# Attention and an MLP on one core: w_out's last quarter in two halves, fewer blank matmuls, and a new order written out as one list

## The chip, the core and the metric

The kernel runs on one core of a Trainium2 chip. The time is that of the device, in microseconds (us) from the start to the end of one execution; the number to compare is the median over repeated runs. The engines are TensorE (PE in the profile, with its weight loads as PEld), VectorE (DVE), ScalarE (ACT), GpSimd (POOL) and SyncE (SP), which here only issues transfers.

## The reference

```
# q, k, v: 8 batches x 8 heads x 576 tokens x 64, float32
def phi(x): r = max(x, 0); return concat([r * cos_w, r * sin_w], -1)   # 128 features
q_p, k_p = phi(q), phi(k)
kv  = einsum('bhsf,bhsd->bhfd', k_p, v)
z   = sum(k_p, axis=2)
num = einsum('bhsf,bhfd->bhsd', q_p, kv)
den = einsum('bhsf,bhf->bhs', q_p, z)[..., None] + 1e-06
x   = (num / den).transpose(0, 2, 1, 3).reshape(4608, 512)
h   = x @ w_in                       # 512 x 2048
out = max(0.01 * h, h) @ w_out       # 2048 x 512
```

`cos_w` and `sin_w` depend on the token's place alone. All inputs and the output are float32; the kernel multiplies in float16.

## The kernel before

The 4608 tokens are worked off in nine groups of 512: the main part of each batch is one group (0 to 7), and the eight batches' last 64 tokens are the ninth. All of w_in (512 x 2048) and w_out (2048 x 512) are loaded in float32 through staging tiles and cast to float16 once; w_in comes in eight pieces (`load_w1(i, cp)`), w_out in four quarters of 128 partitions x 2048 elements (`load_w2(i)`, staging tile `w2st`), each with one cast, `cast_w2(i, eng)`.

A batch goes through these steps. `q_prep` (later `q_part`) makes phi's cosine and sine parts of q (`qp`), `k_pair` (later `k_part`) those of k (`kp`), and `v_pair` (later `v_main`, `v_tail`) casts v, with a column of ones that yields z. In batches 0 and 1 TensorE turns q with a matmul against an identity (`q_turn` into `ps_qt`, `q_turned` copies it out to `qpT`); later a transposing transfer does it. `kv_half` multiplies k and v for one half of the heads (`ps_kvh`), `kv_half_copy` takes it to `kv`; `num_half` multiplies with q (`ps_numh`), `num_div` takes out the denominator (`den`), its reciprocal (`rden`), and divides (`xp`); `x_turn` and `x_turned` turn x into `xT`.

The MLP of group 0 begins in four quads (`quad`), while w_in is still arriving, and goes on in plain products of 512 columns (`ffn1`, eight matmuls a call, `ffn1_out` being the activation on ScalarE; then `ffn2` against w_out, a quarter of its rows a call). Group 1's first product is plain too (`f1_pair`, L833). From group 2 on w_in's product, and from group 1 on w_out's, are made by a scheme with seven block products for eight: `p1` (L882) and `p2` (L975) are groups of four matmuls of 256 columns on sums of blocks that VectorE makes ahead (`w1_sums`, `x_sums`, `g_sums`, `w2_sums`). Between these products PSUM banks are emptied on ScalarE (`seed`, `u_copy`, `lrelu`, `u_lrelu`, `o_copy`) and VectorE (`u_add`, `o_add`). `o_store` sends an output tile out.

TensorE also multiplies blanks: `idle(n, where)` issues n matmuls of a zero tile, 512 columns each, into a PSUM tile `ps_idle` that nobody reads (L190). 19 of them stand ahead of q's first turn, then seven, and eight.

What sets the order: each engine works off its instructions in the order in which the program issues them. The start, up to group 0's `ffn2_out`, is code written out call by call. The rest is a list of calls (`line`), each with a number from the tables in `PLACE`, and is issued in the order of these numbers; `ON` holds a letter for each call that can go to VectorE or ScalarE. Tiles come from pools: an operation that takes a tile of a pool waits until the tile's last reader is done. All loads go through SP's one queue, in program order.

Of the kernel before, what the change touches and what calls it, by code (L numbers as in the profile page):

```python
# [9 lines left out]
dt = mybir.dt  # L10
# [4 lines left out]
J = 4  # L15


@with_exitstack
def kernel(
# [75 lines left out]
    def staged(shape, name, soon=False):  # L95
# [3 lines left out]
    def load_main(nm, src, b, parts=(0, 1), soon=False):  # L99

        if parts[0] == 0:
            st[nm, b] = staged([P, H, J, D], f"{nm}st", soon)
        lo, hi = 4 * parts[0], 4 * parts[-1] + 4
        nc.sync.dma_start(
            st[nm, b][:, lo:hi],
            src[b, lo:hi, 0:MAIN, :].rearrange("h (p j) d -> p h j d", j=J),
        )

    def load_kvtail(nm, src, b):

        t = kvtail.tile([P, H // 2, D], dt.float32, name=f"{nm}tl", tag="kvtail")
        v4 = src[b, :, MAIN:S, :].rearrange("(c o) p d -> o p c d", o=2)
        for o in range(2):
            nc.sync.dma_start(t[o * TAIL : (o + 1) * TAIL], v4[o])
        st[nm + "t", b] = t

    def load_qtail(i):
        if "qt" not in st:
            st["qt"] = staged([P, J, H, D], "qtl")
        for o in range(2):  # L120
            nc.sync.dma_start(
                st["qt"][o * TAIL : (o + 1) * TAIL, i],
                q[2 * i + o, :, MAIN:S, :].rearrange("h p d -> p h d"),
            )

    def load_pair(nm, src, b, lo, hi):
# [3 lines left out]
        flat = src[b].rearrange("h s d -> (h s d)").rearrange("(c x e) -> x c e", x=P, e=JP * D)  # L130
# [3 lines left out]

    def load_k(b):
        load_main("k", k, b)
        load_kvtail("k", k, b)

    def load_v(b):
        load_main("v", v, b)  # L140
        load_kvtail("v", v, b)
# [12 lines left out]
    def load_w1(i, cp):  # L154
# [11 lines left out]
    load_main("q", q, 0, (0,))  # L166
    load_pair("k", k, 0, 0, 1)
    load_pair("k", k, 0, 1, 2)
    load_main("q", q, 0, (1,))
    load_pair("k", k, 0, 2, 4)  # L170
    load_pair("v", v, 0, 0, 2)
    load_pair("v", v, 0, 2, 4)
    load_w1(0, 0)
    load_w1(1, 0)
    load_w1(0, 1)
    load_w1(1, 1)
    load_w1(3, 0)
    load_w1(3, 1)
    load_w1(2, 0)
    load_w1(2, 1)  # L180

    blank = early.tile([P, MAIN], dt.float16, name="blank", tag="blank", bufs=1)
    nc.vector.memset(blank, 0.0)
# [8 lines left out]
    idle(11)  # L192

    ident32 = early.tile([P, P], dt.float32, name="ident32", tag="ident32", bufs=1)
    make_identity(nc, ident32)
    ident = const.tile([P, P], dt.float16, name="ident")
    nc.vector.tensor_copy(ident, ident32)
    w_ang = math.pi / 2.0 / S  # L200
    half_pi = const.tile([P, 1], dt.float32, name="half_pi")
    nc.vector.memset(half_pi, math.pi / 2.0)
    eps = const.tile([P, 1], dt.float32, name="eps")
    nc.vector.memset(eps, 1e-6)
    zero = const.tile([P, 1], dt.float32, name="zero")
    nc.vector.memset(zero, 0.0)
    NA = J + 1 + JP
    pos = const.tile([P, NA], dt.float32, name="pos")
    nc.gpsimd.iota(
        pos[:, 0:J],  # L210
        pattern=[[1, J]],
        base=0,
        channel_multiplier=J,
        allow_small_or_imprecise_dtypes=True,
    )
    for o in range(2):
        nc.gpsimd.iota(
            pos[o * TAIL : (o + 1) * TAIL, J : J + 1],
            pattern=[[1, 1]],
            base=MAIN,  # L220
            channel_multiplier=1,
            allow_small_or_imprecise_dtypes=True,
        )
        nc.gpsimd.iota(
            pos[o * TAIL : (o + 1) * TAIL, J + 1 : NA],
            pattern=[[1, JP]],
            base=0,
            channel_multiplier=JP,
            allow_small_or_imprecise_dtypes=True,
        )  # L230
    cos_t = const.tile([P, NA], dt.float32, name="cos_t")
    sin_t = const.tile([P, NA], dt.float32, name="sin_t")
    nc.scalar.activation(cos_t, pos, AF.Sin, bias=half_pi, scale=w_ang)
    nc.scalar.activation(sin_t, pos, AF.Sin, bias=zero, scale=w_ang)
    warm = const.tile([P, 1], dt.float16, name="warm")
    nc.scalar.activation(warm, zero, AF.Lrelu)

    ones = const.tile([P, H, J, 2], dt.float32, name="ones")
    nc.vector.memset(ones, 1.0)
    vmain = const.tile([P, H, J, NE], dt.float16, name="vmain")  # L240
    nc.vector.tensor_copy(vmain[:, :, :, D:NE], ones)
    vtail = const.tile([P, H // 2, 2, NE], dt.float16, name="vtail")
    nc.gpsimd.memset(vtail, 0.0)
    for o in range(2):
        sl = slice(o * TAIL, (o + 1) * TAIL)
# [671 lines left out]
    def f1_all(g):  # L917
# [16 lines left out]
        if sets == 4:  # L934
            return
# [406 lines left out]
```

## Time and profile before

| | before |
|---|---|
| median of 3 runs | 270.19 us (269.72, 270.19, 270.2) |
| span of the profiled execution | 268.3 us |
| TensorE busy | 262.5 us (98%), 2715 matmuls |
| VectorE busy | 209.2 us (78%) |
| ScalarE busy | 198.6 us (74%) |
| GpSimd busy | 7.7 us (3%) |
| granted TensorE clock | 1.000 |
| chain that ended last | PE 82%, DMA 13%, SP's queue 3%, DVE 1% |

A row of a timeline gives the start, the duration, the engine, the line, the operation with what it writes and reads, the shapes and how many alike follow one another; in brackets stands the idle time just ahead and who ended it. A row of the chain gives the start, the duration and what it was. Of the profiled execution only the span is known, from the first to the last instruction; the time of a run is the longer by what lies around it.

### The profile page before, as it was taken

What the parts mean: (1) busy time and instruction counts of PE and PEld (TensorE: products, weight loads), DVE (VectorE), ACT (ScalarE), POOL (GpSimd) and SP (SyncE); (2) the same over time, 40 slices, a digit from 0 to 9 for tenths busy, and PEclk for the clock granted to TensorE, in tenths of its full rate; (3) what the DMA queues carried; (4) which work ended last, traced back from release to release, by engine and by line L of the source; (5) the groups of instructions that cost most, each with busy time, mean ns of one, the idle gap of its engine ahead of it and who ended that gap; (6) DMA issues with size and microseconds to landing.
All of it is one profiled execution on the core that took longest, in us unless ns stands there. A gap on an engine that the chain in (4) does not pass through costs nothing.

```text
span 268.3 us, 6694 instructions
## 1 busy us (share of the span) xinstructions
PE 262.5 (98%) x2715; PEld 222.9 (83%) x2715; DVE 209.2 (78%) x436; ACT 198.6 (74%) x336; POOL 7.7 (3%) x20
## 2 busy tenths in 40 slices
PE   8999999999999999999999999999999999999994
PEld 3585455566999999999999999999998999999983
DVE  4894998997998998889979967897876674746641
ACT  7675545787989999689878967984996666785621
POOL 2121011000000000000000000000000000000000
PEclk9999999999999999999999999999999999999999
DMA  6999999999999999989899999798893623200116
GB/s 207 377 385 399 380 411 365 276 249 281 209 304 254 234 240 245 264 199 222 221 231 238 198 293 255 140 181 151 135 204 22 138 43 125 112 2 0 78 36 201
DMA packets 82654, 57.05 MB, mean 213 GB/s; under 512 B 54464, under 2 KB 75968, under 8 KB 82112
## 3 DMA queue, kind: packets, MB, share of 16 engines
q1 hardware_dynamic: 82320, 56.37, 84.0%
q8 instruction: 21, 0.34, 0.5%
q10 hardware_dynamic: 304, 0.26, 0.3%
q14 instruction: 9, 0.07, 0.1%
HBM read 36.70 MB, written 9.44 MB: 172 GB/s over the span
## 4 chain that ended last, share of the span: by engine, by line
PE 82%; DMA 13%; SPq 3%; DVE 1%; POOL 0%; issue 0%
PE ps_o L975 34%; PE ps_h L882 18%; PE ps_s L882 14%; DMA w2st<-in_moe_w_out_dram 6%; PE ps_h L833 5%; DMA w1st<-in_moe_w_in_dram 4%; PE ps_num L418 3%; DMA kpr<-in_k_dram 3%; PE ps_kv L317 2%; SPq L131 2%; PE ps_h L975 2%; PE ps_o L543 1%; PE ps_s L975 1%; PE ps_kv L324 1%; DVE w L265 0%; SPq L163 0%
## 5 line engine op out<-in xcount | busy, mean ns | idle before, releaser
L975 PEld LDWEIGHTS <-g 128*128 128x128 f16 x640 | 62.1, 98 | 6.8
L268 DVE TENSOR_TENSOR u<-ps_s,u 128x512 f32<-128x512 f32 x56 | 38.5, 687 | 19.3 <-PE ps_s L882 18.4
L882 PEld LDWEIGHTS <-w 128*128 128x128 f16 x448 | 48.7, 114 | 1.0
L975 PE MATMUL ps_o<-w,g 128*128 128x256 f16 x352 | 46.8, 273 | 0.0
L902 ACT COPY u<-ps_h 128x512 f32<-128x512 f32 x56 | 32.8, 589 | 6.3 <-PE ps_h L882 6.0
L882 PEld LDWEIGHTS <-wa 128*128 128x128 f16 x336 | 34.4, 106 | 1.9
L882 PE MATMUL ps_h<-xw,w 128*128 128x256 f16 x224 | 32.5, 273 | 0.0
L975 PE MATMUL ps_o<-wb,g 128*128 128x256 f16 x232 | 31.5, 273 | 0.0
L909 ACT ACTIVATE g<-u 128x1024 f16<-128x1024 f32 x28 | 29.6, 1060 | 2.3 <-DVE u L268 2.3
L975 PEld LDWEIGHTS <-gs 128*128 128x128 f16 x256 | 24.6, 98 | 2.6
L994 ACT COPY ob<-ps_o 128x512 f32<-128x512 f32 (+1 forms) x32 | 18.0, 561 | 6.0 <-PE ps_o L975 5.8
L892 ACT COPY ps_s<-ps_h 128x512 f32<-128x512 f32 x28 | 16.2, 579 | 6.2 <-PE ps_h L882 5.7
L895 ACT ACTIVATE g<-ps_s 128x512 f16<-128x512 f32 x28 | 16.8, 601 | 5.1 <-PE ps_s L882 4.8
L895 ACT ACTIVATE g<-ps_h 128x512 f16<-128x512 f32 x28 | 16.7, 600 | 5.3 <-PE ps_h L882 5.1
L436 DVE TENSOR_TENSOR xs<-ps_num,rden 128x512 f16<-128x512 f32 x28 | 19.4, 691 | 1.5
L268 DVE TENSOR_TENSOR ob<-ps_o,ob 128x512 f32<-128x512 f32 (+1 forms) x22 | 14.8, 672 | 3.3 <-PE ps_o L975 2.1
L882 PE MATMUL ps_s<-xT,wa 128*128 128x256 f16 x112 | 16.8, 273 | 0.0
L882 PE MATMUL ps_h<-xw,wa 128*128 128x256 f16 x112 | 16.8, 273 | 0.0
L882 PE MATMUL ps_s<-xw,wa 128*128 128x256 f16 x112 | 16.8, 273 | 0.0
L882 PE MATMUL ps_s<-xT,w 128*128 128x256 f16 x112 | 16.8, 273 | 0.0
L882 PE MATMUL ps_h<-xT,w 128*128 128x256 f16 x112 | 16.7, 273 | 0.0
L975 PE MATMUL ps_o<-wb,gs 128*128 128x256 f16 x120 | 16.5, 273 | 0.0
(121 smaller groups left out, 434.5 us busy)
## 6 DMA issues: line engine op xcount, KB each, us to landing
out_dram<-ob SPq DMA_DIRECT2D x16, 512.0 KB, 3.4
qst<-in_q_dram SPq DMA_DIRECT2D x7, 1024.0 KB, 7.0
kst<-in_k_dram SPq DMA_DIRECT2D x6, 1024.0 KB, 8.1
vst<-in_v_dram SPq DMA_DIRECT2D x6, 1024.0 KB, 6.8
w1st<-in_moe_w_in_dram SPq DMA_DIRECT2D x8, 512.0 KB, 11.6
w2st<-in_moe_w_out_dram SPq DMA_DIRECT2D x4, 1024.0 KB, 13.3
vpr<-in_v_dram SPq DMA_DIRECT2D x4, 576.0 KB, 10.7
kpr<-in_k_dram SPq DMA_DIRECT2D x3, 576.0 KB, 11.1
```

The source lines that it names most:

```text
L131: nc.sync.dma_start(st[nm, b][:, lo:hi].rearrange("p c j d -> p c (j d)"), flat[:, lo:hi])
L268: nc.vector.tensor_tensor(out=o, in0=a, in1=b, op=ALU.add)
L418: nc.tensor.matmul(ps[lo:hi, h // 4, (h % 4) * NE : (h % 4) * NE + NM], lhsT=qpT[:, h, lo:hi], rhs=kv[b][:, h, 0:NM],)
L436: nc.vector.tensor_tensor(out=xs, in0=ps[:, :, 0 : 4 * NE].rearrange("p a (b e) -> p a b e", e=NE)[:, :, :, 0:D], in1=rden.rearrange("p (a ...
L833: nc.tensor.matmul(ps, lhsT=w1[m // 4][c // 2][:, c % 2, m % 4 : 512 : 4], rhs=st["xT", g][:, c], start=(c == 0), stop=(c == NKC - 1),)
L882: nc.tensor.matmul(bank[:, p], lhsT=w(c), rhs=x_blocks(g)[n][:, c], start=(fresh and p == 0 and c == 0), stop=(c == 1), skip_group_check=True,
L892: nc.scalar.copy(bank1[bj], bank1[bi])
L895: nc.scalar.activation(st["g" + nm, g][:, 2 * t : 2 * t + 2], bank1[bi], AF.Lrelu)
L902: nc.scalar.copy(st["u", g, t][:, n], bank1[bi])
L909: nc.scalar.activation(st["gt", g][:, :, 1, 2 * t : 2 * t + 2], st["u", g, t], AF.Lrelu)
L975: nc.tensor.matmul(bank, lhsT=st[G2[n], g][:, m, pair * P : (pair + 1) * P], rhs=W2[n](m), start=(fresh and m == 0), stop=(m == NH - 1), s ...
L994: nc.scalar.copy(o_at(g, half_, col, pair), bank_of(bi, pair, pair is None))
```

## The change

The same work is issued in another order, and in finer pieces.

- One text, `ORDER`, lists every call of the program from the first load to the last store, and a loop looks each name up and calls it. The letter at an entry's end names the engine (A ScalarE, V VectorE, G GpSimd). `num_div` is now three entries (`den`, `rec`, `xdiv`; in the halves `hden`, `hrec`, `hdiv`), `kv` is `kv_mm` and `kv_copy`, and loads of tails go by half.
- The last quarter of w_out is loaded in two halves of 128 x 1024 (`ldw2 3 0 2`, `ldw2 3 2 4`) and cast in two, the first on VectorE, the second on ScalarE. The second quarter's cast goes from VectorE to ScalarE.
- Ahead of q's first turn stand 13 blanks (11 and 2) and not 19; the later ones are in pairs between the turns (27 blanks in all, 34 before).
- GpSimd casts no part of batch 0's v (VectorE takes three of the four, ScalarE one) and one piece of w_in, not two; it still casts two parts of batch 1's v.
- TensorE's matmuls other than blanks are the same ones. VectorE has 3 instructions more, ScalarE 1 more, GpSimd 3 fewer.

The core of the diff:

```
-    def load_w2(i):
-        t = staged([P, 4, DM], "w2st", i > 1)
-        nc.sync.dma_start(t, w2v[i])
-        st["w2", i] = t
+    def ldw2(i, lo, hi):
+        if lo == 0:
+            st["w2", i] = staged([P, 4, DM], "w2st", i > 1)
+        nc.sync.dma_start(st["w2", i][:, lo:hi], w2v[i][:, lo:hi])
...
-    def cast_w2(i, eng):
-        copy(eng, w2[:, 4 * i : 4 * i + 4, :], st["w2", i])
+    def cast_w2(i, lo, hi, eng):
+        copy(eng, w2[:, 4 * i + lo : 4 * i + hi, :], st["w2", i][:, lo:hi])
...
-    q_prep(0, 2, 0, 4, ACT)
-    q_prep(0, 0, 0, 4, DVE)
-    q_prep(0, 3, 0, 4, ACT)
-    kp_tiles(0)
-    idle(0, "h1")
-    idle(1, "n")
-    idle(7, "n")
...
-    v_pair(0, 0, 1, POOL)
-    idle(7, "h0")
...
-    PLACE = {
-        "quarters": (
-            10, 112, 260, 408, 557, 696, 826, 959,
...
+ORDER = """
+ld q 0 0 4; ldp k 0 0 1; ldp k 0 1 2; ld q 0 4 8; ldp k 0 2 4; ldp v 0 0 2; ldp v 0 2 4;
+ldw1 0 0; ldw1 1 0; ldw1 0 1; ldw1 1 1; ldw1 3 0; ldw1 3 1; ldw1 2 0; ldw1 2 1; const_all;
+q_part 0 2 0 0 4 A; ldw2 0 0 4; q_part 0 1 1 0 4 V; q_part 0 0 0 0 4 V; q_part 0 1 0 0 4 A;
+q_part 0 3 1 0 4 A; kp_tiles 0; k_pair 0 0 0; idle 2 h0; k_pair 0 0 1; q_part 0 2 1 0 4 A;
+q_turn 0 2 0 4 o; q_part 0 3 0 0 4 V; q_turn 0 3 0 4 o; idle 2 h1; k_pair 0 1 0;
+q_turned 0 3 0 4 V; q_part 0 0 1 0 4 A; q_turn 0 0 0 4 o; q_turned 0 0 0 4 A; k_pair 0 1 1;
+idle 2 h1; q_part 0 3 0 4 8 V; q_part 0 0 1 4 8 V; q_turned 0 2 0 4 V; q_turn 0 1 0 4 o;
...
+ffn2 0 1 4 8; q_turn 1 0 0 8 h1; kv_half 1 0 h0; cast_w2 2 0 4 V; ffn2 0 0 4 8;
...
+kv_half 1 1 h1; ffn2 0 2 8 12; kv_half_copy 1 1 A; cast_w2 3 2 4 A; hden 1 1 0 V;
+cast_w2 3 0 2 V; hrec 1 1 0; hdiv 1 1 0; num_half 1 1 1 h1; ffn2 0 2 12 14; hden 1 1 1 V;
...
+lrelu 4 11 0 2; g_sums 3 3 4 8; p2 3 2 1 0 1 0; seed 4 1 2; p1 4 0 6 0 0; p1 4 0 5 3 1;
+u_copy 4 0 0 0; v_tail 5 1 V; p1 4 1 6 1 0; k_part 5 4 1 V; k_part 5 2 0 A; k_part 5 4 0 V;
+v_tail 5 0 V; u_copy 4 1 0 1; p1 4 0 7 0 0; ld q 6 0 8; p2 3 2 1 1 1 0; p2 3 2 0 1 1 0;
...
+    words = {"A": ACT, "V": DVE, "G": POOL, "S": nc.sync}
+    for n, row in enumerate(ORDER.replace("\n", " ").split(";")):
+        if row.strip():
+            name, *args = row.split()
+            OPS[name](*(int(a) if a.isdigit() else words.get(a, a) for a in args))
```

The last two lines of `ORDER` before the loop show how a bank's round trip reads there: `p1 4 0 6 0 0` is the last product into bank 0, `u_copy 4 0 0 0` empties it on ScalarE, two groups of matmuls (`p1 4 0 5` and `p1 4 1 6`, in other banks) stand between, and `p1 4 0 7 0 0` writes bank 0 again.

Where it moves instructions, three places. VectorE ahead of its first division, in batch 0 (`kpr` is k as loaded, `vpr` v as loaded, `den` and `rden` the denominator and its reciprocal, `xp` the quotient). Before:

```order
L282 SCALAR_TENSOR_TENSOR kp<-kpr,cos_t 128x9x64 [waits DMAHW4_49]
L282 SCALAR_TENSOR_TENSOR kp<-kpr,sin_t 128x9x64
L265 COPY qpT<-ps_qt 128x512 [waits PE_49]
L282 SCALAR_TENSOR_TENSOR kp<-kpr,cos_t 128x9x64
L282 SCALAR_TENSOR_TENSOR kp<-kpr,sin_t 128x9x64
L433 TENSOR_SCALAR den<-ps_numh 128x8 [waits PE_49]
L435 RECIPROCAL rden<-den 128x8 [waits DVE_49]
L436 TENSOR_TENSOR xp<-ps_numh,rden 128x2x256 [waits DVE_49]
```

And now:

```order
L508 SCALAR_TENSOR_TENSOR kp<-kpr,cos_t 128x9x64 [waits DMAHW4_49]
L508 SCALAR_TENSOR_TENSOR kp<-kpr,sin_t 128x9x64
L491 CAST vpair<-vpr 128x9x64 [waits DMAHW5_49]
L491 CAST vpair<-vpr 128x9x64
L508 SCALAR_TENSOR_TENSOR kp<-kpr,sin_t 128x9x64
L508 SCALAR_TENSOR_TENSOR kp<-kpr,cos_t 128x9x64
L491 CAST vpair<-vpr 128x9x64 [waits DMAHW6_49]
L662 TENSOR_SCALAR den<-ps_numh 128x8 [waits PE_49]
L666 RECIPROCAL rden<-den 128x8 [waits DVE_49]
L483 TENSOR_SCALAR qp<-qst,cos_t 128x4x64
L670 TENSOR_TENSOR xp<-ps_numh,rden 128x2x256 [waits DVE_49]
```

Three casts of v and a part of q now stand ahead of the first division, and a copy of turned q has gone.

SP's queue from w_out's first quarter on (`w2st` w_out, `kpr`, `qst` and `vpr` batch 1's k, q and v; numbers tell buffers apart). Before:

```order
L163 DMA w2st_363<-in_moe_w_out_dram 128x2048
L131 DMA kpr_372<-in_k_dram 128x2x576
L163 DMA w2st_427<-in_moe_w_out_dram 128x2048
L104 DMA qst_452<-in_q_dram 128x8x256
L131 DMA vpr_503<-in_v_dram 128x2x576
L163 DMA w2st_506<-in_moe_w_out_dram 128x2048
L131 DMA kpr_372<-in_k_dram 128x2x576
L131 DMA vpr_503<-in_v_dram 128x2x576
```

And now:

```order
L411 DMA w2st_206<-in_moe_w_out_dram 128x2048
L411 DMA w2st_437<-in_moe_w_out_dram 128x2048
L359 DMA qst_471<-in_q_dram 128x8x256
L386 DMA kpr_507<-in_k_dram 128x2x576
L386 DMA vpr_529<-in_v_dram 128x2x576
L411 DMA w2st_544<-in_moe_w_out_dram 128x2048
L386 DMA kpr_507<-in_k_dram 128x2x576
L386 DMA vpr_529<-in_v_dram 128x2x576
L411 DMA w2st_576<-in_moe_w_out_dram 128x1024 x2
```

The first piece of batch 1's k has moved behind w_out's second quarter and q, and the last quarter is two transfers.

ScalarE around group 0's activations (`g`), with `ps_h` the products of w_in. Before:

```order
L263 CAST w_0_1_106<-w1st 128x1024 [waits DMAHW1_49]
L536 ACTIVATE g<-ps_hq 128x4x256 [waits PE_49] x2
L515 ACTIVATE g<-ps_h 128x1024 [waits PE_49] x4
L515 ACTIVATE g<-ps_h 128x1024
L515 ACTIVATE g<-ps_h 128x1024 [waits PE_49]
L263 CAST vpair<-vpr 128x9x64 [waits DMAHW3_49,Activation_49]
L263 COPY qpT<-ps_qt 128x1024 [waits PE_49]
```

And now:

```order
L489 CAST w_0_1_106<-w1st 128x1024 [waits DMAHW1_49]
L489 CAST w_1_1_108<-w1st 128x1024 [waits DMAHW2_49]
L776 ACTIVATE g<-ps_hq 128x4x256 [waits PE_49] x2
L755 ACTIVATE g<-ps_h 128x1024 [waits PE_49] x5
L489 CAST w_113<-w2st 128x2048 [waits DMAHW0_49]
L481 ACTIVATE qp<-qst,sin_t 128x8x64 [waits DMAHW1_49,DVE_49,Activation_49]
L755 ACTIVATE g<-ps_h 128x1024 [waits PE_49]
L481 ACTIVATE qp<-qst,cos_t 128x8x64
L489 COPY qpT<-ps_qt 128x1024 [waits PE_49]
```

A cast of w_out's second quarter and a part of batch 1's q stand ahead of the last of group 0's six activations, and another piece of w_in ahead of the first.

More of the change, by code (lines that the diff above doesn't have):

```diff
@@ L231 @@
[L231 to L240, printed above, removed]
@@ new lines, in const_all @@
+        nc.scalar.activation(cos_t, pos, AF.Sin, bias=half_pi, scale=w_ang)
+        nc.scalar.activation(sin_t, pos, AF.Sin, bias=zero, scale=w_ang)
+        nc.scalar.activation(warm, zero, AF.Lrelu)
+        nc.vector.memset(ones, 1.0)
+        nc.vector.tensor_copy(vmain[:, :, :, D:NE], ones)
+        nc.gpsimd.memset(vtail, 0.0)
+        for o in range(2):
+            sl = slice(o * TAIL, (o + 1) * TAIL)
+            nc.vector.tensor_copy(vtail[sl, :, o, D:NE], ones[sl, 0:4, 0, :])
+        nc.gpsimd.memset(vpair[:, :, :, D:NE], 1.0)
@@ L784, in w2_sums, with late_pools @@
+    def late_pools():
+        first.close()
+        late.append(pool("late", 1))
+        gq.append(pool("gq", 2))
+        tpool.append(pool("t", 2))
+        opool.append(pool("out1", 1))
+        for s in (1, 2, 4):
+            wb[s] = late[0].tile([P, NH, N2], dt.float16, name=f"wb{s}")
     def w2_sums(i, s):
```

990 lines of the change are left out of this document (407 added, 583 removed), and 52 rows, old and new, of the table PLACE.

## The prediction

> **What bounds the kernel now.** The page's head first: how long, and which engine is full.
>
> ```profile
> span 268.3 us, 6694 instructions
> PE 262.5 (98%) x2715; PEld 222.9 (83%) x2715; DVE 209.2 (78%) x436; ACT 198.6 (74%) x336; POOL 7.7 (3%) x20
> ```
>
> TensorE is busy for 262.5 of 268.3 us, so no order of the same work can gain more than a part of 5.8 us. The profiled execution has its span only; the median of the runs is 270.19, and I carry the 1.9 us around the span unchanged. So the sum below is one of differences, made inside the span and added to 270.2. A measurement can tell about 0.2%, which is 0.54 us.
>
> The chain of waits says where the span is not TensorE's own. Early on it runs through loads:
>
> ```profile
> 2.74 7.40 DMA kpr<-in_k_dram
> ...
> 29.64 14.88 DMA w2st<-in_moe_w_out_dram
> 44.55 1.24 DVE w L265
> 50.65 8.63 PE ps_h L833 x40
> 120.56 2.62 PE ps_o L975 x24
> ...
> 205.54 1.00 PE ps_h L882 x8
> ...
> 214.78 0.98 PE ps_o L975 x8
> 217.88 0.98 PE ps_o L975 x8
> ```
>
> The last quarter of w_out lands at 29.64 + 14.88 = 44.52, VectorE casts it for 1.24, and only then go the four matmuls at 45.83. Behind that the chain is TensorE alone: 8.63 / 40 = 0.216 us for a matmul of 512 columns, 2.62 / 24 = 0.109 for one of 256. Three pieces of eight take 0.98 to 1.00 where 8 x 0.109 = 0.87: 0.13 + 0.11 + 0.11 = 0.35 us, the only crumbs of the chain behind 66 us. TensorE's timeline shows the same places and how small the gaps are:
>
> ```profile
> 1.19 6.49 PE L190 MATMUL ps_idle<-blank 128*128 128x512 f16 x19 [1.19 <-DVE blank L183]
> 7.51 0.61 PE L405 MATMUL ps_qt<-ident,qp 128*128 128x128 f16 x8
> ...
> 12.67 0.75 PE L349 MATMUL ps_kvh<-vpair,kp 64*128 64x65 f16 x36 [0.42 <-POOL vpair L265]
> ...
> 15.61 0.40 PE L475 MATMUL ps_xth<-ident,xp 128*128 128x128 f16 x4 [0.37 <-DVE xp L436]
> ...
> 20.68 8.80 PE L506 MATMUL ps_h<-xT,w 128*128 128x512 f16 x40
> ...
> 38.08 0.74 PE L349 MATMUL ps_kvh<-vpair,kp 64*128 64x65 f16 x36
> ...
> 45.26 0.42 PE L453 MATMUL ps_numh<-kv,qpT 128*128 128x65 f16 x8
> 45.83 1.02 PE L543 MATMUL ps_o<-w,g 128*128 128x512 f16 x4
> ...
> 50.48 8.80 PE L833 MATMUL ps_h<-xT,w 128*128 128x512 f16 x40
> ```
>
> Bracketed are the waits: 0.42 for v, 0.37 for the first division. The eight matmuls at 45.26 take 0.26 (the pitch of the rows of eight), so there is a gap of 0.31 ahead of 45.83. These are all the gaps worth a number that the edits touch.
>
> **The blanks.** 19 blanks stand ahead of q's first turn now, 13 afterwards. ScalarE's and the weight load's timelines price that:
>
> ```profile
> 6.22 0.49 ACT L255 ACTIVATE qp<-qst,sin_t 128x256 f16<-128x256 f32 x1
> 5.00 0.15 PEld L190 LDWEIGHTS <-blank 128*128 128x128 f16 x1 [0.28 <-issue]
> 6.00 1.17 PEld L190 LDWEIGHTS <-blank 128*128 128x128 f16 x6 [0.34 <-issue]
> ```
>
> The fourth q part of ScalarE ends at 6.71. The blanks go one in 0.43 until about 5.0 and one in 0.216 behind that, so 13 of them end at about 6.1 and the turn can start at about 6.77, not 7.51: 0.74 us sooner. What that buys is nothing by itself, since the first kv (12.67) waits for v, whose load is in the same place in its queue. Cost taken: 0.
>
> **GpSimd's casts.** Batch 0's v goes from GpSimd, ScalarE, ScalarE, GpSimd to VectorE, VectorE, ScalarE, VectorE. The rows:
>
> ```profile
> 11.71 0.91 POOL L265 CAST vpair<-vpr 128x576 f16<-128x576 f32 x1 [9.00 <-DMA vpr<-in_v_dram]
> 13.20 0.70 POOL L265 CAST vpair<-vpr 128x576 f16<-128x576 f32 x1 [0.58 <-DMA vpr<-in_v_dram]
> 18.64 0.68 DVE L265 CAST w<-w1st 128x1024 f16<-128x1024 f32 x1
> 10.41 0.34 DVE L257 TENSOR_SCALAR qp<-qst,sin_t 128x256 f16<-128x256 f32 x1
> 10.68 0.75 DVE L282 SCALAR_TENSOR_TENSOR kp<-kpr,cos_t 128x576 f16<-128x576 f32 x1
> 11.35 0.75 DVE L282 SCALAR_TENSOR_TENSOR kp<-kpr,sin_t 128x576 f16<-128x576 f32 x1
> 14.43 0.15 DVE L433 TENSOR_SCALAR den<-ps_numh 128x8 f32<-128x8 f32 x1
> 14.86 0.69 DVE L436 TENSOR_TENSOR xp<-ps_numh,rden 128x512 f16<-128x512 f32 x1
> ```
>
> A cast of 1024 elements takes VectorE 0.68 and one of 2048 takes 1.24, so one of 576 takes about 0.68 - 448 x 0.56 / 1024 = 0.43 (an estimate), some 0.41 in a row. Walk VectorE's new order from v's landing at 11.7: two casts end at 12.5, two k_pairs of 0.67 (10.68 to 11.35) at 13.9, the third cast at 14.3; then den and the reciprocal (14.43 to 14.86: 0.43), and a q part of 0.27 (10.41 to 10.68) stands ahead of the division, which starts at 15.0 where it started at 14.86. kv itself starts at 12.2 to 12.95 against 12.67. The division leads to x's turn (15.61), the quads and w_in's products (20.68), between which TensorE is full. So 20.68 becomes 20.8: **+0.1**, between -0.45 (kv as early as v allows, and all that hangs on it) and +0.4 (all three casts on the path beyond GpSimd's 0.91).
>
> **Loads and casts from 20 to 46 us.** SP now issues w_out's second quarter and batch 1's q ahead of batch 1's first k. The landings of before are the starts of those who waited for them:
>
> ```profile
> 27.22 1.23 DVE L265 CAST w<-w2st 128x2048 f16<-128x2048 f32 x1 [1.09 <-DMA w2st<-in_moe_w_out_dram]
> 31.24 1.23 DVE L265 CAST w<-w2st 128x2048 f16<-128x2048 f32 x1 [0.18 <-DMA w2st<-in_moe_w_out_dram]
> 34.23 0.49 DVE L257 TENSOR_SCALAR qp<-qst,cos_t 128x512 f16<-128x512 f32 x1 [0.42 <-DMA qst<-in_q_dram]
> 35.74 0.67 ACT L263 CAST vpair<-vpr 128x576 f16<-128x576 f32 x1 [2.61 <-DMA vpr<-in_v_dram]
> 17.43 1.05 ACT L263 CAST w<-w1st 128x1024 f16<-128x1024 f32 x1
> 20.01 1.94 ACT L536 ACTIVATE g<-ps_hq 128x1024 f16<-128x1024 f32 x2 [1.54 <-PE ps_hq L525]
> ```
>
> From 34.23 to 35.74 one piece of k or v landed: 1.5 us each. So w_out's second quarter lands at 31.24 - 1.5 = 29.7, q at 32.7, and k at 34.2, where it came at about 27.22 + 1.5 = 28.7 before (estimates all). Three consequences.
>
> ScalarE takes one more piece of w_in, 1.05, ahead of the quads' activations, where it idled 1.54: hidden; without that room the activations would be late by 1.05, which the first of w_in's products would not feel, since they use other banks.
>
> ScalarE now casts w_out's second quarter: two times 1.05 at most, so 2.0 (estimate), behind the activation of the fifth eight of w_in's products (their end at 20.8 + 40 x 0.216 = 29.4, and some 1.05 for as many elements as a cast): from 30.5 to 32.5. TensorE wants it after 48 matmuls of w_in and 8 of the first quarter, at 20.8 + 56 x 0.216 = 32.9. Hidden, by 0.4; uncovered it would cost at most the 1.5 by which the load is moved.
>
> VectorE's row to the first kv of batch 1 (38.08) is now: four q parts of 0.4 from 32.7 to 34.3, a k_pair, two q parts, three k_pairs, which makes 4 x 0.67 + 2 x 0.4 = 3.5, so 37.8, and TensorE is there at 38.1. Hidden by 0.3, with k landing at 34.2 as the uncertain term: each 0.1 us later than 34.5 stops TensorE by 0.1. Taken: 0, and up to +1.3 should q land no sooner than before, at 34.23.
>
> The last quarter: with the same bytes ahead, its first half lands half a quarter sooner (1.3 of 2.5 us), at about 43.2; VectorE's cast of 0.68 is done by 43.9 to 44.6, and the second half, landed at 44.5, is cast by ScalarE (1.05) by 45.6 to 45.85. TensorE wants the halves at 45.5 and 46.6. The gap of 0.31 closes: **-0.3**. If VectorE or ScalarE take the halves late, nothing is lost beyond the gap of today.
>
> **Mid-run, 50 to 265 us.** The same matmuls in another order. What the order alone tells: between the last matmul into a PSUM bank and the next that needs it emptied stand at least two groups of four matmuls, 8 x 0.109 = 0.87 us; this least distance occurs twice before, and 20 times after (18 in mid-run, 2 in the tail). How tight that is, rows of before show:
>
> ```profile
> 72.48 0.60 PE L882 MATMUL ps_h<-xw,wa 128*128 128x256 f16 x4
> 73.12 0.59 ACT L902 COPY u<-ps_h 128x512 f32<-128x512 f32 x1
> 73.80 0.60 PE L882 MATMUL ps_h<-xw,w 128*128 128x256 f16 x4
> L909 ACT ACTIVATE g<-u 128x1024 f16<-128x1024 f32 x28 | 29.6, 1060 | 2.3 <-DVE u L268 2.3
> ```
>
> The bank is full at 73.08, the copy starts at 73.12 and ends at 73.71, and TensorE goes on at 73.80, its natural time: a reserve of 0.09 where ScalarE is free. At 14 of the 18 places the instruction ahead of the copy on ScalarE has its input at least a group (0.44) sooner, and I take 0. At four, an activation of 1.06 or a long q part stands right ahead; I take 0.1 to 0.2 at each, 0.5 in all, against most of today's crumbs of 0.35 us, which another order need not have: **+0.2**, between -0.35 (all crumbs gone) and 18 x 0.12 = +2.1. The tail's order after the last product is the same: 0.
>
> **The sum:** +0.1 - 0.3 + 0 + 0.2 = 0.0, so 270.2, within 0.2%.
>
> **The rivals.**
>
> A, slower: ScalarE is late at the two-group distances. It decides once the copy starts over 0.09 after its bank is full. For it: 20 places against 2, ScalarE at 74%; against it: in most the instruction ahead is ready early. At 18 x 0.12 it costs 2.1: 272.3; at half of them 1.1.
>
> B, slower: the loads of batch 1 land no earlier, VectorE's k_pairs end late, and TensorE stops at batch 1's first kv by up to 1.3, while the last quarter's gap goes: 270.2 + 1.3 - 0.3 = 271.2. For it: VectorE's row there has 0.3 of cover; against it: loads run back to back, so the pieces should land in the order of issue.
>
> C, faster: v's casts on VectorE start kv at 12.2, 0.45 sooner, TensorE keeps that up to w_in's products, which start at 20.2, the gap of 0.31 closes and the crumbs of 0.35 go: 270.2 - 1.1 = 269.1; with half the crumbs 269.3. For it: GpSimd's 0.91 is the very wait of 12.67. Against it: VectorE gets three casts and a q part ahead of its first division.
>
> D, slower: with fewer blanks TensorE's clock falls before 12 us. In before a blank goes in 0.43 at first and in 0.216 from about 5.0 on, so a slow phase doubles each matmul; if the first kv, the nums and x's turns, some 2 us of matmuls, went at half speed, +1.7: 271.9. For it: of the stretch from 6.1 to 12.6 TensorE is busy about two thirds afterwards, nearly all of it before. Against it: the longest gap left there is some 0.7 us. [...]
>
> Should the halves do nothing, because VectorE takes the first one late, the forecast is 270.5, still no change.
>
> **The numbers.** The forecast has 0.33, its own range is 269.7 to 270.7. A has 0.20, B 0.10, D 0.06, C 0.31. Faster by over 0.2% is C, 0.31; no change 0.33; slower is A, B and D, 0.36. The range takes C's full sum, 269.1, with the 0.1 by which the two casts are uncertain, so 269.0, and A's, 272.3; left out are the stretches beyond both, and where A and B or A and D come together, not 2 in 10.
>
> **What would show it.** In the new profile: q's first turn near 6.8 and w_in's 40 matmuls near 20.8 (20.2 is C); no wait at the first kv of batch 1 near 38 (one of a microsecond is B); no gap ahead of the last quarter near 45.5, and the next group's first product near 50.3; PSUM waits on TensorE between 50 and 265 summing to about 0.7 us (two or more is A); weight loads of the first kv and nums at today's pitch (twice that is D). The forecast is wrong if w_in's products start before 20.4 or if mid-run waits exceed 1.3 us.

## The result and the profile after

The changed kernel takes 272.58 us (median of 5 runs, 272.06 to 272.9) against 270.2 (5 runs of before): the ratio is 1.0084, with an interval of 1.0067 to 1.01. It is slower by 2.4 us. The profiled execution took 272.45 us, with a span of 270.6 where before had 268.3. The page's head after:

```profile
span 270.6 us, 6669 instructions
PE 262.8 (97%) x2708; PEld 222.1 (82%) x2708; DVE 208.2 (77%) x439; ACT 202.6 (75%) x337; POOL 6.6 (2%) x17
```

TensorE's busy time is what it was, 262.8 for 262.5, at a granted clock of 1.0. So the 2.3 us are waits of TensorE. Its timeline up to group 1, the rows that answer to those of before:

```profile
1.19 4.89 PE L416 MATMUL ps_idle<-blank 128*128 128x512 f16 x13 [1.19 <-DVE blank L438]
6.98 0.40 PE L627 MATMUL ps_qt<-ident,qp 128*128 128x128 f16 x4 [0.91 <-ACT qp L481]
...
12.76 0.46 PE L575 MATMUL ps_kvh<-vpair,kp 64*128 64x65 f16 x18 [0.44 <-DVE vpair L491]
13.41 0.46 PE L575 MATMUL ps_kvh<-vpair,kp 64*128 64x65 f16 x18 [0.20 <-DVE vpair L491]
...
16.54 0.40 PE L715 MATMUL ps_xth<-ident,xp 128*128 128x128 f16 x4 [0.20 <-DVE xp L670]
...
21.62 10.52 PE L746 MATMUL ps_h<-xT,w 128*128 128x512 f16 x48
...
39.02 0.75 PE L575 MATMUL ps_kvh<-vpair,kp 64*128 64x65 f16 x36
...
46.21 0.42 PE L687 MATMUL ps_numh<-kv,qpT 128*128 128x65 f16 x8
46.47 1.02 PE L783 MATMUL ps_o<-w,g 128*128 128x512 f16 x4
...
51.13 8.87 PE L900 MATMUL ps_h<-xT,w 128*128 128x512 f16 x40
```

The first kv starts as late as before (12.76 for 12.67), x's first turn 0.93 later (16.54 for 15.61), and w_in's products 0.94 later (21.62 for 20.68). Batch 1's kv at 39.02 has no wait. Between the eight matmuls at 46.21 and w_out's last quarter at 46.47 there is no gap any more, and group 1's product starts 0.65 later than before (51.13 for 50.48). What is lost behind it is in TensorE's small waits, of which these three pairs are examples. A group of four takes 0.44, so the second row of each pair would start 0.44 behind the first if nothing held it:

```profile
78.92 0.60 PE L943 MATMUL ps_h<-xw,w 128*128 128x256 f16 x4
79.72 0.60 PE L943 MATMUL ps_s<-xT,wa 128*128 128x256 f16 x4 [0.21 <-DVE u L494]
...
87.16 0.60 PE L943 MATMUL ps_h<-xw,w 128*128 128x256 f16 x4
87.78 0.41 PE L640 MATMUL ps_num<-kv,qpT 128*128 128x65 f16 x8
...
175.05 0.60 PE L943 MATMUL ps_h<-xw,w 128*128 128x256 f16 x4
175.93 0.60 PE L943 MATMUL ps_s<-xw,wa 128*128 128x256 f16 x4 [0.29 <-DVE u L494]
```

The excess is 0.36, 0.18 and 0.44. Behind group 1's product, the places where a matmul starts over 0.025 us later than its usual distance behind the one ahead (0.216 for 512 columns, 0.109 for 256) sum to 1.76 us, against 0.13 before. Left out in both are the four nums of the last 64 tokens, which cost some 0.8 in all before and after alike; one of before, then one of after, with the group behind it:

```profile
205.09 0.45 PE L418 MATMUL ps_num<-kv,qpT 128*64 128x65 f16 x16
205.47 0.63 PE L882 MATMUL ps_h<-xT,w 128*128 128x256 f16 x4
```

```profile
204.16 0.45 PE L640 MATMUL ps_num<-kv,qpT 128*64 128x65 f16 x16
204.54 0.63 PE L943 MATMUL ps_h<-xw,w 128*128 128x256 f16 x4
```

A ledger from TensorE's timelines, used for the experiments too (us; "end" is the end of TensorE's last matmul in the trace; "w_in" and "group 1" are the first products with w_in of groups 0 and 1):

| kernel | x's first turn | w_in | group 1 | w_in to group 1 | group 1 to end |
|---|---|---|---|---|---|
| before | 15.61 | 20.68 | 50.48 | 29.80 | 214.23 |
| after | 16.54 | 21.62 | 51.13 | 29.51 | 215.94 |
| difference | +0.93 | +0.94 | +0.65 | -0.29 | +1.71 |

So the profiled 2.3 is +0.94 up to w_in, -0.29 up to group 1, +1.71 from there on, and less than 0.1 the other way in the tail.

### The profile page after: what moved, and what is told of

It reads as the page before. It is cut to its first block, busy times and chain, and to the rows that moved or that the text cites. A ratio compares the mean times of both kernels' runs of the same rounds, so it can differ in the third digit from the quotient of the medians.

```text
span 270.6 us, 6669 instructions
## 1 busy us (share of the span) xinstructions
PE 262.8 (97%) x2708; PEld 222.1 (82%) x2708; DVE 208.2 (77%) x439; ACT 202.6 (75%) x337; POOL 6.6 (2%) x17
## 4 chain that ended last, share of the span: by engine, by line
PE 84%; DVE 9%; DMA 4%; issue 1%; SPq 0%; ACT 0%; DVEq 0%
PE ps_o L1009 29%; PE ps_h L943 16%; PE ps_s L943 13%; PE ps_o L783 5%; PE ps_h L900 5%; PE ps_h L746 4%; DMA qst<-in_q_dram 3%; PE ps_num L640 2%; PE ps_kv L545 2%; DVE kp L508 2%; DMA kpr<-in_k_dram 2%; PE ps_h L1009 2%; PE ps_s L1009 1%; PE ps_hq L765 1%; DVE gs L497 1%; DVE kp L483 1%
## 5 line engine op out<-in xcount | busy, mean ns | idle before, releaser
L1009 PE MATMUL ps_o<-w,g 128*128 128x256 f16 x352 | 45.3, 273 | 0.0
L1009 PE MATMUL ps_o<-wb,g 128*128 128x256 f16 x232 | 32.2, 273 | 0.0
```

The lines of the kernel that those rows point to most:

```text
L1009: nc.tensor.matmul(bank, lhsT=st[G2[n], g][:, m, pair * P : (pair + 1) * P], rhs=W2[n](m), start=bool(fresh and m == 0), stop=(m == NH - 1 ...
```

## The experiments

My theory from the two traces: VectorE's three casts of v delay the start, and in mid-run VectorE is late for banks that TensorE wants back. Its rivals: the start's loss is GpSimd's and not the casts'; the mid-run loss comes out of the start, as work that is merely shifted; ScalarE is late at the two-group distances (rival A); the clock falls with fewer blanks (rival D). Each kernel's time stands beside runs of before on its own chip (medians 270.11 to 270.2).

### Which stretch loses: four kernels with one order ahead of a joint and the other behind it

The first two change over at 50 us, where group 0's w_out product ends:

```
 start_before:  ...order of before... ; late_pools ; ...changed ORDER...
 start_after:   ...changed ORDER...   ; late_pools ; ...order of before...
```

> The start of the kernel before (up to group 0's outputs, its loads, casts and blanks) and behind it the changed order from 50 us on. Theory 1, two separate losses: the start loses 0.65 us (the first of group 1's products at 51.13 in place of 50.48), the order from 50 us on loses 1.7 by late VectorE and ScalarE; so this kernel is at 270.2 + 1.7 = 271.9. Rival: the later part waits only because the new start hands its loads and buffers on late; then this kernel is at about 270.2 to 270.5.

> The changed start and behind it the order of the kernel before. Theory 1: only the start's loss is left, 270.2 + 0.65 = 270.85. Rival (the later waits come from the new start): about 272.2 to 272.6, as the changed kernel.

Measured: start_before 274.69 us (six runs from 273.83 to 276.31), 1.0179 [1.0148, 1.0211]; start_after 271.55, 1.0045 [1.0032, 1.0059]. Neither adds up directly, since the joint itself stalls TensorE: 2.29 behind 59 us in the first (its kv waits for VectorE's cast of v), 0.55 + 0.37 + 0.25 in the second. So the joint was moved to 66 us, behind group 1's w_in product:

```
 start_before66:  ...order of before... ; open_banks ; ...changed ORDER...
 start_after66:   ...changed ORDER...   ; open_banks ; ...order of before...
```

> The changed order up to 66 us (where the banks of the seven-product scheme are opened) and the kernel before's from there on; six instructions of the first part that the other order has later go at the joint. In the first pair of mixed kernels the joint at 50 us made waits of its own (2.4 and 0.6 us). Theory 1: the waits of 0.05 to 0.4 us belong to the changed order behind 66 us, so none of them is here, and only the start's loss is left: 270.1 + 0.3 to 0.6 = 270.4 to 270.7. Rival: they come from the state that the start leaves, and the time is near 271.6 or above.

> The kernel before's order up to 66 us and the changed one from there on, with eleven entries (loads of batch 3 among them) that the changed order has earlier put at the joint. Theory 1: the waits near 79 and 87 us and the small ones behind are all here, 270.1 + 1.4 = 271.5, and more where batch 3's loads, now later, are waited for. Rival: 270.1 to 270.5.

Measured: start_after66 272.87, 1.0106 [1.009, 1.0122]; start_before66 273.94, 1.0147 [1.0132, 1.0162]. The joints stall here too, in the first at one place, as its waits on TensorE show (us in all, times, longest):

```profile
PE ps_num L616 <- ACT xT L465: 1.8, 1, 1.8
```

All four times lie above what theory 1 expected of them, by 0.7 to 2.8 us, so the times alone don't decide; the joints' stalls have to be taken off. The joint of start_after66 costs 1.94 us on the timeline, the three stalls of start_before66 0.97 + 0.56 + 0.14 = 1.67. Taken off the stretch from group 1 to the end, the ledger splits cleanly:

| kernel | behind the joint | group 1 to end | joint's stalls | rest |
|---|---|---|---|---|
| start_after | old order | 215.29 | 1.17 | 214.12 |
| start_after66 | old order | 216.13 | 1.94 | 214.19 |
| start_before | new order | 218.15 | 2.29 | 215.86 |
| start_before66 | new order | 217.57 | 1.67 | 215.90 |

Before has 214.23 and after 215.94. The mid-run loss goes with the order behind 66 us, whatever the start: the rival that it is a shifted start falls. What the start alone costs is less certain. By start_after66 it is 272.87 - 1.94 - 270.17 = 0.76 us, by start_after 271.55 - 1.17 - 270.2 = 0.18. The single pair of profiles in the ledger overstates it: w_in began at 20.68 to 21.33 in the six profiles with the old order there (before, start_before, start_before66, before_halves, halves_v, before_blanks; mean 20.95), and at 21.14 to 21.65 in the six with the changed one (after, start_after, start_after66, q7_early, u_add_early, mid_fixed; mean 21.43). Before's 20.68 is the earliest of them all. So about 0.5 of the 0.94 goes with the order, and the rest with the run.

With the old start the same place as in after stalls, here for 0.54, on TensorE's timeline of start_before66:

```profile
80.10 0.60 PE L920 MATMUL ps_h<-xw,w 128*128 128x256 f16 x4
81.08 0.60 PE L920 MATMUL ps_s<-xT,wa 128*128 128x256 f16 x4 [0.38 <-DVE u L471]
```

### The start: who casts batch 0's v

VectorE's timeline in after, from v's first cast to the first division:

```profile
11.96 1.41 DVE L491 CAST vpair<-vpr 128x576 f16<-128x576 f32 x2
13.28 0.75 DVE L508 SCALAR_TENSOR_TENSOR kp<-kpr,sin_t 128x576 f16<-128x576 f32 x1
...
14.61 0.74 DVE L491 CAST vpair<-vpr 128x576 f16<-128x576 f32 x1
15.28 0.15 DVE L662 TENSOR_SCALAR den<-ps_numh 128x8 f32<-128x8 f32 x1
...
15.59 0.30 DVE L483 TENSOR_SCALAR qp<-qst,cos_t 128x256 f16<-128x256 f32 x1
15.80 0.69 DVE L670 TENSOR_TENSOR xp<-ps_numh,rden 128x512 f16<-128x512 f32 x1
```

VectorE is in one row from 11.96 to the division at 15.80, and a cast takes 0.66 in a row (0.74 by itself), not the 0.41 of the prediction. Three times 0.25 is most of the 0.8 between the 15.0 forecast and 15.80; that the first cast began at 11.96 and not 11.7 is made up for by a denominator, reciprocal and q part that took 0.52 (15.28 to 15.80) and not 0.70.

v_gpsimd puts three of v's casts back to GpSimd and ScalarE, in the new order:

```
-v_pair 0 0 1 V; ... v_pair 0 1 2 V; ... v_pair 0 3 4 V
+v_pair 0 0 1 G; ... v_pair 0 1 2 A; ... v_pair 0 3 4 G
```

> The changed kernel with batch 0's four v casts on GpSimd, ScalarE, ScalarE, GpSimd as before, every entry in its place. Theory: VectorE's three casts, 2.0 us in all by the trace, are what delays the first division from 14.86 to 15.80; with them gone the division is back near 14.9 and w_in's products near 20.7: 272.6 - 0.9 = 271.7. Rival: the k_pairs' and turns' new order or the fewer blanks delay it: 272.4 to 272.6.

Measured: 272.31 us, 1.0075 [1.0059, 1.0092]. No gain; TensorE now waits 1.63 for GpSimd, as GpSimd's and TensorE's timelines of v_gpsimd show:

```profile
11.44 2.56 POOL L469 CAST vpair<-vpr 128x576 f16<-128x576 f32 x2 [8.73 <-DMA vpr<-in_v_dram]
```

```profile
13.44 0.75 PE L553 MATMUL ps_kvh<-vpair,kp 64*128 64x65 f16 x36 [1.63 <-POOL vpair L469]
```

Of the 2.56, the first cast took 1.95 (11.44 to 13.39), beside k_pairs that VectorE worked through without a gap until 12.87; the second took 0.66, with VectorE idle. Before needed 0.91 for its first. So GpSimd is no way out in this order, and the run doesn't say whether the casts alone or the whole new order ahead of them delay the division: it came at 15.78, as in after. The old order meets the same collision when VectorE's k_pairs fall later: in halves_v they ran from 11.33 to 12.75, GpSimd's two casts, which began at 11.59, took 2.28 together, kv waited for the first until 13.32 (12.67 in before), and w_in began at 21.33, the latest of the old starts.

v_merged casts two parts of v in one instruction on VectorE, with the order left as it is:

```
-v_pair 0 0 1 V; ... v_pair 0 1 2 V
+v_pair 0 0 2 V
```

> The changed kernel with the first two v casts of batch 0 (128 x 9 x 64 each, on VectorE) made as one of 128 x 2 x 9 x 64. [...]

My estimate for the one cast was 0.67, half of the 1.33 that the two take, which no row showed, and with that gain of 0.65 a time of 271.95; without it 1.27 for the cast and 272.5.

Measured: 272.03 us, 1.007 [1.0052, 1.0088]. VectorE's timeline, and GpSimd's below it:

```profile
11.81 0.76 DVE L469 CAST vpair<-vpr 128x1152 f16<-128x1152 f32 x1
...
13.82 0.75 DVE L469 CAST vpair<-vpr 128x576 f16<-128x576 f32 x1
...
14.79 1.00 DVE L461 TENSOR_SCALAR qp<-qst,cos_t 128x256 f16<-128x256 f32 x1
15.71 0.68 DVE L648 TENSOR_TENSOR xp<-ps_numh,rden 128x512 f16<-128x512 f32 x1
```

```profile
14.61 1.04 POOL L469 CAST w<-w1st 128x1024 f16<-128x1024 f32 x1 [11.90 <-DMA w1st<-in_moe_w_in_dram]
```

The cast of 1152 elements takes 0.76, as long as one of 576 (0.75 at 13.82): the half size ran at half the rate. A part of v is 9 rows of 64 that go to rows of 66; the merged cast has two such blocks. But the division starts at 15.71, hardly sooner: the q part ahead of it took 1.00 where it took 0.30 in after. It ran while GpSimd cast w_in's piece (14.61 to 15.65), and ended only behind it, at 15.79; GpSimd's cast took 1.04, as in after. What the merging gained was lost in that one instruction. That the median is near the 271.95 expected is therefore luck, and its interval overlaps that of after: the 0.65 that was to come from the start is not in the start.

start_fixed adds the obvious repair to v_merged, the q part ahead of the last cast and so ahead of GpSimd's:

```
+q_part 0 1 0 4 8 V;
 v_pair 0 3 4 V; ... hrec 0 1 0;
-q_part 0 1 0 4 8 V;
 cast_w1 0 0 G
```

> The changed kernel with batch 0's first two v casts as one and the q part that stood between the first reciprocal and the first division moved ahead of the last v cast. With the merged cast alone VectorE was 0.67 us sooner at its first den, but the q part behind it then took 1.00 in place of 0.30 while GpSimd cast a piece of w_in, and the division came at 15.71. Theory: what the start loses is these VectorE instructions alone; the division now starts near 15.15 and w_in's products near 20.9, 0.55 sooner: 272.58 - 0.55 = 272.0. Rival: the last v cast, later by 0.27, makes kv's second half the bound, and nothing is gained: 272.5.

Measured: 272.22 us, 1.0075 [1.0055, 1.0095]. VectorE's timeline of start_fixed:

```profile
12.71 0.76 DVE L469 CAST vpair<-vpr 128x1152 f16<-128x1152 f32 x1
...
14.72 0.34 DVE L461 TENSOR_SCALAR qp<-qst,cos_t 128x256 f16<-128x256 f32 x1
...
16.07 0.69 DVE L648 TENSOR_TENSOR xp<-ps_numh,rden 128x512 f16<-128x512 f32 x1
```

The q part is back at 0.34, and from v's first cast to x's first turn it is 4.11 us (12.71 to 16.82), where after has 4.58 and v_merged 4.64; before has 3.90 (11.71 to 15.61). In this profile VectorE's row ran late: a q part at 9.71 waited 0.48 for its load, and v's first cast began at 12.71, where after's began at 11.96. That hides the gain in the absolute times, and the median shows none beyond its interval. The shorter stretch is shown by the rows; a gain in time is not.

### The last quarter: halves alone

before_halves is before with only the halves; halves_v casts both on VectorE:

```
-ldw2 3 0 4;     cast_w2 3 0 4 V
+ldw2 3 0 2; ldw2 3 2 4;    cast_w2 3 2 4 A; cast_w2 3 0 2 V     (before_halves)
+ldw2 3 0 2; ldw2 3 2 4;    cast_w2 3 0 2 V; cast_w2 3 2 4 V     (halves_v)
```

> The kernel before with w_out's last quarter loaded in two halves, the first cast on VectorE and the second on ScalarE. Theory: the gap of 0.31 us ahead of the last quarter's matmuls closes, as in the changed kernel, and nothing else moves: 270.2 - 0.3 = 269.9. Rival: in the old order the cast that ScalarE takes delays its den behind it, or the gap is only moved to the second half: 270.2.

> The kernel before with w_out's last quarter in halves, both cast on VectorE. With the second half on ScalarE its den behind the cast came 1 us late and TensorE waited 0.28 for the division instead of 0.31 for the cast. Theory: with both on VectorE ScalarE's den is in time, the first half is cast by 44.7 and the second by 45.3, and the gap closes: 270.1 - 0.3 = 269.8. Rival: the division behind the second cast comes later by its 0.6 and the wait stays: 270.1.

Measured: before_halves 270.33, 1.0013 [0.9997, 1.003]; halves_v 270.2, 0.9998 [0.9982, 1.0015]. The halves by themselves bring nothing. In before_halves the gap only moves: ScalarE's timeline, then TensorE's:

```profile
44.60 1.05 ACT L465 CAST w<-w2st 128x1024 f16<-128x1024 f32 x1
45.55 0.27 ACT L636 ACTIVATE den<-ps_numh,eps 128x8 f32<-128x8 f32 x1
```

```profile
46.91 0.43 PE L663 MATMUL ps_numh<-kv,qpT 128*128 128x65 f16 x8 [0.28 <-DVE xp L646]
```

The cast stands ahead of the denominator on ScalarE, the division comes late, and TensorE waits 0.28 there. In halves_v w_in to group 1 is 29.44, but its start was late (w_in at 21.33), and so it is 29.44 in start_before too, with whole quarters and a start at 20.84. Where TensorE comes some 0.2 later, the whole quarter is ready as well: the -0.29 of after's ledger is the gap swallowing part of the late start, not a gain of its own.

### The blanks alone

```
-idle 19 ahead of q's first turn, idle 7 h0, idle 8
+idle 13 ahead of q's first turn, idle 2 h0, idle 2 and 2
```

> The kernel before with 13 blanks ahead of q's first turn (19) and two where seven, four and four stood. Theory: nothing hangs on them, the first kv waits for v: 270.2 within 0.1. Rival: the turns come sooner and VectorE's copies with them, a gain of 0.2 to 0.4; or the clock falls before 12 us and the weight loads of kv go at half the pace, a loss of over 1.

This kernel has 19 blanks in all, where the changed one has 27, so it is the harder test. Measured: 270.28 us, 1.0001 [0.999, 1.0012]. Nothing in the time, yet rival D's mechanism was there. Its rows by stretch (from:to, length, busy time of PE, PEld, DVE, ACT, POOL, then the granted clock), and two rows of TensorE's timeline:

```profile
10.00:12.00 2.00, 0.49 (x6) 0.32 (x5) 2.00 (x5) 1.63 (x5) 0.74 (x1) 1.00 1.03 403
12.00:14.00 2.00, 1.93 (x56) 1.87 (x56) 1.30 (x2) 1.53 (x4) 1.07 (x2) 0.76 1.04 389
14.00:16.00 2.00, 2.00 (x48) 1.74 (x46) 1.79 (x5) 1.42 (x4) 1.04 (x1) 0.50 1.05 389
```

```profile
12.07 0.74 PE L550 MATMUL ps_kvh<-vpair,kp 64*128 64x65 f16 x36 [1.46 <-POOL vpair L466]
14.37 1.17 PE L550 MATMUL ps_kvh<-vpair,kp 64*128 64x65 f16 x36
```

With TensorE busy 0.49 of the 2 us ahead, all of it turns of q, the clock went to 0.76 and then 0.50, and the second kv took 1.17 where the first took 0.74. Six of twelve runs had a mean clock of 0.993 or 0.994 over the span, which is 0.6% of 268 us, or 1.6 us lost, as much as some 3 us at a clock of 0.50 would lose (an estimate); they are no slower than the rest. In the profiled one v had come early (GpSimd's first cast at 11.26), w_in still began at 20.90, and the gap ahead of the last quarter took the 0.2 that was left; of the other five no trace is kept. Here 1.46 us without a matmul, in a thinly used stretch (0.49 of 2 us), preceded the drop; how long a wait or how thin a use it takes no run shows. In after's profile the clock is 1.00 in every stretch from 4 to 20 us, and its run with the lowest mean clock, 0.997, is its fastest, 272.06; so D is no part of its 2.4.

### Mid-run: the single waits

Three waits of after were tried. At 175 us VectorE is late, and its timeline shows why; at 79 us it simply has too much ahead:

```profile
77.38 0.69 DVE L491 CAST vmain<-vst 128x1024 f16<-128x1024 f32 x1
77.99 0.48 DVE L483 TENSOR_SCALAR kp<-kst,cos_t 128x512 f16<-128x512 f32 x1
78.38 0.69 DVE L491 CAST vmain<-vst 128x1024 f16<-128x1024 f32 x1
78.98 0.69 DVE L494 TENSOR_TENSOR u<-ps_s,u 128x512 f32<-128x512 f32 x1
...
173.72 0.49 DVE L483 TENSOR_SCALAR qp<-qst,sin_t 128x512 f16<-128x512 f32 x1 [1.77 <-DMA qst<-in_q_dram]
...
175.19 0.69 DVE L494 TENSOR_TENSOR u<-ps_s,u 128x512 f32<-128x512 f32 x1
```

The addition at 78.98 (`u_add`) empties a PSUM bank. Its last input, ScalarE's copy of `u`, was done at 77.97, but a k part and a cast for batch 3 stand ahead of it, so it starts 1.0 later. ScalarE's row:

```profile
77.37 0.60 ACT L963 COPY u<-ps_h 128x512 f32<-128x512 f32 x1 [0.20 <-PE ps_h L943]
```

In before the same addition stands in a VectorE row that is just as full, but TensorE's next matmul into the bank comes only 1.5 us after it is done (78.90 to 80.41). VectorE's row of before, then TensorE's:

```profile
78.22 0.68 DVE L268 TENSOR_TENSOR u<-ps_s,u 128x512 f32<-128x512 f32 x1
```

```profile
80.41 0.60 PE L882 MATMUL ps_s<-xT,wa 128*128 128x256 f16 x4
```

At 87.78 it is the num that waits: the division whose bank it takes ends on VectorE at 87.64. The profile names ScalarE's copy into `ps_s` instead, which ended a little later, at 87.69, and which the num does not need.

q7_early issues batch 7's q load sooner, ahead of two transposing transfers; u_add_early puts the addition at 78.98 ahead of the three entries that belong to batch 3; mid_fixed adds the move of the num at 87.78 behind one more group of matmuls (one, not the three of its expectation); all_fixed joins start_fixed and mid_fixed:

```
 q_part 6 2 1 0 8 V;
+ld q 7 0 8;                       (q7_early)
 ...
 q_transpose_dma 6 2; q_transpose_dma 6 3; ...
-ld q 7 0 8;

 u_copy 2 0 1 0;
+u_add 2 0 1 3;                    (u_add_early, mid_fixed, all_fixed)
 k_part 3 3 0 V; ... v_tail 3 0 A; v_main 3 4 8 V;
-u_add 2 0 1 3;

-num_mm 3 0;
 ...
 p2 1 5 1 1 1 0;
+num_mm 3 0;                       (mid_fixed, all_fixed)
```

> The changed kernel with batch 7's q load moved ahead of batch 6's last two q transposes on SP's queue, right behind the last q part that frees its buffer. Theory: VectorE's wait of 1.77 us for that load (171.9 to 173.7) goes, u_add is in time and TensorE's stall of 0.44 at 175.5 goes: 272.58 - 0.44 = 272.1. Rival: u_add is late there for other work ahead of it, or the earlier load delays the q transposes behind it and the next nums wait: 272.5 or more.

> The changed kernel with the first u_add of group 2 right behind its u_copy, ahead of two casts of v and a k part on VectorE. Theory: the bank that u_add empties is free a microsecond sooner and TensorE's stall of 0.36 at 79.3 goes: 272.58 - 0.36 = 272.2. Rival: the casts of v are then late for batch 3's kv and TensorE waits there as long: 272.5.

> The changed kernel with group 2's first u_add right behind its u_copy, and batch 3's first num three groups of matmuls later, behind the division whose bank it needs. Theory: these two places, where TensorE waits for VectorE, are 0.37 + 0.18 of the order's loss; u_add alone gave 0.6 in the span behind 50 us: 272.58 - 0.75 = 271.8. Rival: the num's wait moves on to the division behind it: 272.0 as with u_add alone, or more.

> Both of these edits together. If the start's loss and the order's loss are separate, their gains add: 272.58 - 0.55 - 0.75 = 271.3, with about 1 us left over the kernel before in the small waits of 0.05 to 0.10. If they are not, less than 1.0 is gained.

q7_early: 274.22 us, 1.0143 [1.0123, 1.0164], 1.6 slower than after. Its timeline of TensorE:

```profile
170.59 0.43 PE L618 MATMUL ps_num<-kv,qpT 128*128 128x65 f16 x8 [2.02 <-DMA qpT<-qp]
```

The load ahead of the transposes made them late by 2 us: on SP's one queue the load had stood behind them for a reason, as the rival had it. The wait of 1.77 at 173.72 was moreover an accident of after's profiled run; the 0.44 at 175 is in no other profile of this order.

u_add_early: 271.77, 1.0059 [1.0041, 1.0077], 0.8 below after's median, with an interval that overlaps after's. Its profile shows how little of that is the edit's: w_in began early, at 21.16, and from group 1 to the end it is 215.35, which is 0.59 less than in after, but 0.44 of that is the accident at 175. What is left is 0.15: the 0.36 at 79 is gone, and batch 3's kv behind it waits 0.20 instead. The 0.6 that mid_fixed's expectation gives this edit holds the accident. mid_fixed: 271.94, 1.0067 [1.0048, 1.0087]. The num's wait is gone, and a new one of 0.23 stands four groups behind it (89.42 to 90.09), for an addition of VectorE. all_fixed: 271.87, 1.0066 [1.0046, 1.0086]. No repair gets back to before; each single wait of VectorE that is taken away comes back in part at VectorE's next due instruction.

## Why the prediction was wrong

It forecast no change, 269.0 to 272.3; the time is 272.58.

**"GpSimd's casts: +0.1"** is the first step that failed: it was +0.94 in the profile, some 0.5 by the means of six profiles each, and 0.2 to 0.8 by the times of start_after and start_after66, in which the closing of the last quarter's gap is already counted. The mechanism was right (three casts and a q part ahead of the first division) and its price wrong. I scaled 0.43 from the weights' casts of 1024 and 2048 elements (0.68 and 1.24); the shape cast here took 0.74, as the k_pair of the same shape did in the prediction's own rows (0.75). My upper bound of +0.4 rested on that same 0.43. Why nine rows of 64 took 0.74 and twice nine rows 0.76 (v_merged) no run shows. It is not the rows of 66 that cost: the casts of `vmain` at 77.38 and 78.38 write such rows as well, sixteen of them, and take 0.69 for 1024 elements.

**"Mid-run: +0.2"** is the second, and the larger: +1.71 in the profile, of which 0.44 is that run's accident. Without the accident v_merged and start_fixed, which have the same order there, take 215.52 and 215.50 from group 1 to the end, 1.3 more than before. I priced only ScalarE at the two-group distances. There it costs even less than the 0.5 taken: four late starts of 0.07, 0.03, 0.02 and 0.02. I did not walk VectorE's order for the additions that empty PSUM banks and for the divisions, where 0.36 and 0.18 are lost in single places, nor ScalarE's at the longer distances. Of the 1.3 us of waits over 0.025 that after's profile has beside the accident, VectorE's instruction ended last for about 0.87 (the two above and five of 0.03 to 0.10), ScalarE's for about 0.44 (eight of 0.03 to 0.09). What makes the smallest of them late stays open.

The other half of that term, the crumbs of 0.35 in before, was not there to be had: they are the groups behind three of the four nums of the last 64 tokens, and after has them as well. So the lower bound of -0.35, and the same 0.35 in rival C, had no ground.

**"The last quarter: -0.3"**: the gap went and the size was right, but it is not a gain of the halves: it goes wherever the start is later by some 0.2, and in before_halves it came back as a wait of 0.28 for a division.

**"The blanks: 0"** held in the time: 6.98 for q's first turn (forecast 6.77), 1.0001 for the blanks alone.

**"Loads and casts from 20 to 46 us: 0"** held. VectorE's first q part of batch 1 started at 32.22 (forecast 32.7), ScalarE's cast of w_out's second quarter ran 31.38 to 33.27, and neither kv at 39.02 nor w_out's product waited. One thing did slip there without cost, a cast of v on GpSimd:

```profile
35.31 2.58 POOL L491 CAST vpair<-vpr 128x576 f16<-128x576 f32 x1 [19.66 <-DMA vpr<-in_v_dram]
```

**The rivals.** A gave nearly the measured time, 272.3, by a mechanism that the trace hardly has: at the two-group distances ScalarE is late for some 0.15 us in all, and VectorE is late for two thirds of the recurring waits. B did not happen (q landed by 32.22). C did not happen: kv started no sooner and the small waits grew. D happened in before_blanks without cost, and not in after. What I had named as making the forecast wrong, mid-run waits over 1.3 us, is what came. The range reached up to A's 272.3 because it took one loss at a time; here a late start and late banks came together. The some 0.5 and 1.3 us that recur make less than the 2.4 of the medians; how often the accident of 0.44 stood in the runs without a profile is not known.

## What to carry to other kernels

When a new order is priced, walk each engine that empties PSUM banks, and for each bank set the time at which that engine's row lets it start against the time at which TensorE comes back: VectorE's row was full at 78 us before and after, and only after did TensorE come back too soon. Price an instruction by the row of the same shape, even where it is another operation, before scaling a row of the same operation with another shape: here the k_pair's 0.75 was right for the cast of 0.74, and the scaled 0.43 was not. And where a late start ends in front of a gap, the gap's disappearance is not a gain.

## What the runs showed of the hardware

A VectorE cast from float32 to float16 of nine rows of 64 into rows of 66 took 0.74 us (after), of two times nine rows 0.76 (v_merged), and of 1024 elements in sixteen such rows 0.69 (after).

Instructions of VectorE and GpSimd took longer beside each other in these rows: a GpSimd cast of 576 elements took 0.66 while VectorE stood idle (v_gpsimd), and 1.95 (v_gpsimd) and 2.58 (after) while VectorE worked through k_pairs in a row. The other way round, a VectorE q part rose from 0.30 to 1.00 beside a GpSimd cast of 1024 (v_merged), and a k_pair from 0.75 to 1.21 (13.29 in before) beside GpSimd's cast of 576 at 13.20. It is not so in every row: in after GpSimd's cast of 1024 at 14.61 took 1.04, as at 14.29 in v_gpsimd with VectorE idle until 15.24, and VectorE's cast of v at 14.61 took 0.74, as long as VectorE's cast at 14.98 in start_fixed (0.75), where GpSimd stood idle until 15.60. What decides it no run shows.

In before_blanks the granted clock fell to 0.76 (12 to 14 us) and 0.50 (14 to 16) after 1.46 us without a matmul, in a stretch that was a quarter busy (0.49 of 2 us).

The same load landed at different times in different runs: the first piece of batch 0's v, issued at 3.29 in before and in before_blanks, ended GpSimd's wait for it at 11.71 and 11.26 us, and in start_before, with the same start, at 12.19. Differences of half a microsecond at the start are judged from the stretch between two instructions, or from medians, not from one profile's absolute times.
